# Between two mixture layers: evacuations and transposes moved up, three weight splits moved down, filler matmuls of another kind

## The chip, the core and the metric

The kernel runs on one core of a Trainium2 chip. The metric is the device time of one execution in microseconds (us), taken as the median of repeated runs. The core has five engines that run their own instruction streams and wait for each other through semaphores: TensorE (PE, with its weight loads shown as PEld), VectorE (DVE), ScalarE (ACT), GpSimd (POOL) and SyncE (SP), which here only issues DMAs. [...]

## What is computed

Three layers follow each other. An attention with a window of 32 and 32 global tokens gives 4 * (512 + 32) = 2176 tokens of 512 numbers, which the kernel handles as 17 tiles of 128. A mixture layer with a rational activation follows, then a layer with eight experts of which each token takes the one with the highest logit:

```
h = x @ w_in;  g = P(h) / (Q(h) + 1e-06);  x2 = g @ w_out           # first mixture layer
logits = normed(x2) @ normed(expert_emb).T / tau
expert_idx = argmax(logits);  gate_w = softmax(logits)[expert_idx]
for e in range(8):                                                   # second mixture layer
    mask = expert_idx == e
    out[mask] = gate_w[mask] * (relu(x2[mask] @ w1[e]) @ w2[e])
```

## The kernel before

The matrix products run in a three-term form: each float32 operand is split into a high part (rounded to fp32r) and a low part (the rest), and hi*hi, hi*lo and lo*hi are added. So every weight has to be split before it is used: ACT copies out the high part, DVE or POOL subtracts it to get the low part.

**The first mixture layer** (`moe1`) runs over blocks of tokens (`BLOCKS`, two of 512 tokens and three of 384) and slices of the hidden width. `gemm1` makes h, `poly`, `inv` and their kin make g on ACT, DVE and POOL, and `gemm2` adds to four accumulators in PSUM. When a token tile's sum is complete, `evac` (L1029) adds it on DVE to x2, and `final` writes x2 to DRAM (L1040, on SP's queue), transposes it on PE (L1043, four 128x128 transposes into tile tp) and copies the transpose out on ACT (L1050).

**Logits and ranks.** When a block has all its transposes, `logits` multiplies by the expert embeddings on PE (L1073) and ACT copies the result to `part` (L1078); `logits2` folds it into tile lp (L1084). A generator `pick` then does the block's ranks on DVE: maximum (L280, tile zm), one-hot (L281 to L289), running counts by matmuls of constants on PE (L294 to L298), then ranks (L309 to L321). `next(g)` runs it one step on; `for _ in g` runs it to its end. `norm` (L1058) sums squares on ACT; `norms` turns them into lengths (L331 to L342).

**After the last slice** (n = NK, L1165 on) this is written out by hand. Three token tiles (14, 15, 16) still have to be evacuated and transposed, and the ranks of blocks 2, 3 and 4 have to be done in their order, since each block's counts (`cum`) go on from the one before.

**The weights of expert 0 and 1.** In the same stretch the second layer's first weights are split. They come in eight chunks of 512 KB in the staging buffers `stg`: 0 to 3 are w1, 4 to 7 are w2. `first_hi` (L1226, ACT) makes the high part of a chunk, `first_lo` (L1231, DVE) the low part. For the chunks in `EARLY` = (0, 2) `first_lo` also starts the load of expert 1's chunk into the buffer just freed (L1233, on SP's queue). The others' low parts of w2 are made by DVE after the second layer has begun (L1624).

**Routing** (`route`) finishes the last `pick`, places each expert's tokens in slots (`place`, L489 to L508), and looks up by 17 small matmuls (`table`, L480) which token sits in which slot. From that come idx (L459) for the first gather of 128 rows of x2 by POOL's indirect DMA (L514), and scat (L463) for the scatters. `warm` (L468) puts transposes of the identity on PE ahead of and behind the table, whose results nobody reads.

**The second mixture layer** (`moe2`) is one critical block in which each engine has its own program with hand-placed semaphores. Every engine enters it through one branch (L1736, SP through a NO_OP at L1266) that waits for everything that came before: each DMA queue's semaphore at its last value, and each engine's. Then PE transposes the first gathered rows (L1373, d_x), runs 6 more transposes of `warm` (called at L1453), and multiplies (L1418 for a half-filled unit, L1404 for a full one, tile d_h; L1444 the second product, tile d_o). DVE turns the table's second use into gates (L1609 to L1613) and makes low parts (L1571); POOL makes others (L1676).

Nothing but the order in the source decides the order on each engine here; waits between engines are derived from what is read and written.

Of the kernel before, what the change touches and what calls it, by code (L numbers as in the profile page):

```python
# [19 lines left out]
P = 128  # L20
# [64 lines left out]
class Kernel:  # L85
# [331 lines left out]
    def route(self):  # L417
        tc, nc = self.tc, self.nc
        V, T = nc.vector, nc.tensor
        NS = NSLOT  # L420
        self.idx = self.wpool.tile([P, NS], I32, name="idx")
        self.scat = self.wpool.tile([P, NS], I32, name="scat")
        self.gate = self.big.tile([P, NS], F32, name="gate")
        self.tab = self.wpool.tile([1, NROW * NU], I32, name="tab")
        sel = self.wpool.tile([P, NTILE * NS // 2], F32, name="sel")
        self.sel = sel.bitcast(F16).rearrange("p (a b) -> p a b", b=NS)
        self.gs = sel[:, 0:3 * NS].rearrange("p (a b) -> p a b", b=NS)

        def run(gens, steps=10 ** 9):
            while gens and steps:  # L430
                g = gens.pop(0)
                if next(g, run) is not run:
                    gens.append(g)
                steps -= 1

        with ExitStack() as ctx:
            rp = ctx.enter_context(tc.tile_pool(name="r_sb", bufs=1))
            last = self.psteps.pop()
            while self.total is None:
                next(last)  # L440
            nu = rp.tile([P, E], I32, name="nu")
            ub = rp.tile([P, E], F32, name="ub")
            od = rp.tile([1, E], I32, name="od")
            tail = chain(self.nsteps, self.gates())
            wb = self.bank("s", "wb")
            self.warm(wb, 20)
            run([self.place(rp, nu, ub, od), last, islice(tail, 7)])
            rhs = self.table_rhs(self.xgt, 1)
            self.table_mul(V, rhs, 0, self.tok)
            t = self.lp[:, TB:TB + NS]  # L450
            self.table(T, t, rhs)
            self.warm(wb, 36)
            back = [self.slots(rp, ub, nu, od), tail]
            run(back, 3)

            up = rp.tile([P, NS], F32, name="up")
            none = rp.tile([P, NS], F32, name="none")
            V.tensor_scalar(up, t, 0.0, -1.0, ALU.is_gt, ALU.mult)
            V.scalar_tensor_tensor(self.idx, t, float(MID), up, ALU.add, ALU.add)  # L459
            self.gather(nc.gpsimd, 0, 0)  # L460
            run(back)
            V.tensor_scalar(none, t, 0.0, float(OOB), ALU.is_equal, ALU.mult)
            V.tensor_tensor(self.scat, self.idx, none, ALU.add)  # L463

    def warm(self, out, n):

        for _ in range(n):
            self.nc.tensor.transpose(out[:, 0:P], self.ident, self.ident)  # L468

    def table_rhs(self, t, n):  # L470
        return t[:, 0:NTILE * n * NSLOT // 2].bitcast(F16).rearrange("p (a j b) -> p a j b", j=n, b=NSLOT)
# [47 lines left out]
    def attention(self, ctx):  # L519
# [315 lines left out]
        }  # L835
        warm = one.tile([P, 512], F32R, name="warm")
        nc.scalar.copy(warm, vgs[0].rearrange("p a b c -> p (a b c)"))

        def heat(d, n):
            for _ in range(n):  # L840
                nc.tensor.matmul(d, warm[:, 0:P], warm, start=True, stop=True)
# [151 lines left out]
    def moe1(self, ctx, kctx, xctx):  # L993
# [8 lines left out]
        def gemm2(k):  # L1002
            g, (t0, n), f = k
            gh, gl = G.pop(k)
            wh, wl = self.w[f, 1]
            grp = GROUPS[g]
            first, last = f == grp[0], f == grp[-1]
            for i in range(n // P):
                tt = t0 // P + i
                if first:  # L1010
                    acc[tt] = self.bank("o", "o")
                o = acc[tt]
                gs = slice(i * P, (i + 1) * P)
                nc.tensor.matmul(o, gh[:, gs], wh[:, DM:], start=first, stop=False)  # L1014
                nc.tensor.matmul(o, gh[:, gs], wl[:, DM:], start=False, stop=False)  # L1015
                nc.tensor.matmul(o, gl[:, gs], wh[:, DM:], start=False, stop=last)  # L1016
                if last:
                    done.append((g, tt, o))

        def evac(g, tt, o):  # L1020
            if g == 0:
                (nc.scalar.copy if tt % 2 else nc.vector.tensor_copy)(self.x2[tt], o)
            elif tt % 2 and g < len(GROUPS) - 1:
                nm = ("junk", "part")[tt // 2 % 2]
                x = wk.tile([P, DM], F32, tag=nm, name=nm, bufs=1)
                nc.scalar.copy(x, o)
                nc.gpsimd.tensor_tensor(self.x2[tt], x, self.x2[tt], ALU.add)
            else:
                nc.vector.tensor_tensor(self.x2[tt], o, self.x2[tt], ALU.add)  # L1029
            if g == len(GROUPS) - 1:  # L1030
                fin.append(tt)

        def bank(nm):
            if n == NK:
                turn.append(turn.pop(0))
            return self.bank("s" if turn[0] else "t", nm)

        def final(tt):
            x2 = self.x2[tt]
            nc.sync.dma_start(self.x2_dram[tt * P:(tt + 1) * P, :], x2)  # L1040
            tp = bank("tp")
            for c in range(NDC):
                nc.tensor.transpose(tp[:, c * P:(c + 1) * P], x2[:, c * P:(c + 1) * P], self.ident)  # L1043
            bi, (a, b) = block_of(tt)
            if tt == a:

                old = BLOCKS[(bi - 1) % 3][0] // (2 * P)
                XT[bi] = self.st_raw if bi == 0 else [t.rearrange("p a b -> p (a b)") for t in pair[old:old + 2]]
            j = tt - a
            nc.scalar.copy(XT[bi][j // 2][:, j % 2 * DM:(j % 2 + 1) * DM], tp)  # L1050
            late.append(tt)
            if tt == b - 1:
                full.append(bi)

        def norm():
            for tt in late:
                junk = wk.tile([P, 512], F32, tag="junk", name="junk", bufs=1)
                nc.scalar.activation(junk, self.x2[tt], AF.Square, accum_out=self.ss[:, tt:tt + 1])  # L1058
            late.clear()

        def block_of(tt):
            bi = next(i for i, x in enumerate(BLOCKS) if tt * P < sum(x))
            return bi, (BLOCKS[bi][0] // P, sum(BLOCKS[bi]) // P)

        def logits(bi):

            w = BLOCKS[bi][1]
            xt = XT.pop(bi)
            tp = bank("lt")[:, :w]
            for i in range(0, w, 2 * P):  # L1070
                x = xt[i // (2 * P)].rearrange("p (a b) -> p a b", b=DM)[:, 0:min(2, (w - i) // P)]
                for c in range(NDC):
                    nc.tensor.matmul(  # L1073
                        tp[c * WIN:(c + 1) * WIN, i:min(i + 2 * P, w)], self.ent[:, c], x[:, :, c * P:(c + 1) * P],
                        start=True, stop=True, tile_position=(0, c * WIN),
                    )
            part = wk.tile([P, 512], F32, tag="part", name="part", bufs=1)[:, :w]
            nc.scalar.copy(part, tp)  # L1078
            return part
# [19 lines left out]
        done, fin, full, late, parts, XT, turn = [], [], [], [], [], {}, [0, 1, 1]  # L1099
# [7 lines left out]
        for n in range(PRE, NK):  # L1107
# [52 lines left out]
            g, blk, f = ks[n - LAG + 1]  # L1160
# [18 lines left out]
        g = self.psteps[-1]  # L1179
        while next(g) is None:  # L1180
            pass
        self.first_lo((0, 2))
        part = logits(full.pop())
        norm()
        gemm2(ks[-1])
        next(g)
        for _ in g:
            pass
        for d in done:
            evac(*d)  # L1190
        self.first_hi((1, 3))
        self.psteps.clear()
        logits2(bl - 1, part)
        g = self.psteps.pop()
        while next(g) is None:
            pass
        while fin:
            final(fin.pop(0))
        for _ in g:
            pass  # L1200
        self.first_lo((1, 3))
        part = logits(full.pop())
        norm()
        self.nsteps = self.norms()
        next(self.nsteps)
# [46 lines left out]
    def moe2(self, ctx):  # L1252
# [5 lines left out]
        po = [pp.tile([P, 512], F32, name=f"d_o{i}") for i in range(2)]  # L1258
# [7 lines left out]
        with tc.tile_critical():  # L1266
# [20 lines left out]
            def base(nm, j, half):  # L1287
                return sum(incs[nm][h] for _, h in order[:order.index((j, half))])
# [45 lines left out]
            with nc.Block() as block:  # L1334
# [27 lines left out]
                def _(E):  # L1362
# [13 lines left out]
                    def second(j):  # L1376
                        either(E, two[j], lambda: tx_(j, 1), lambda: E.sem_inc(tx[1], 1))
# [72 lines left out]
                    n = val(ET.PE, 6, 0, NU_MIN, NU)  # L1450
                    ahead(0)
                    second(0)
                    self.warm(po[0], 6)  # L1453
                    for j in range(NU):
                        if 0 < j < NU - 1:
                            ahead(j + 1)
# [283 lines left out]
```

## Time and profile before

| | us |
|---|---|
| median of 3 runs (901.66 to 907.16) | 904.59 |
| the profiled execution | 896.24 |
| its span, first to last instruction | 894.3 |
| in it, from the last product of the first layer to the first expert product | 578.9 to 603.7 |

The page's first section gives each engine's busy time as a share of the span. The chain of waits is followed back from the last instruction, at each step to what released it. A timeline row gives start, duration, engine, line, operation, output and inputs, count, and in brackets the idle time before it and what ended that. In the table by windows the column PEclk is the granted clock. "Issue" is a wait for nothing that the profile shows.

### The profile page before, as it was taken

The numbers are of one execution on the slowest core, as the hardware profiler recorded it, in microseconds if no ns is written. First come the engines' busy times: TensorE is split into PE (matmuls) and PEld (weight loads), VectorE is DVE, ScalarE is ACT, GpSimd is POOL, SyncE is SP. The second block draws the span as 40 slices with busy tenths as digits, with TensorE's granted clock in tenths as the row PEclk, the third lists the DMA queues.
The fourth block names the chain that finished last, engine by engine and source line by source line (L and its number), as shares of the span: only waits on it lengthen the run. The fifth ranks groups of instructions, "written<-read, shape, count | busy, mean of one in ns | idle before, by whom it ended". The sixth has DMA issues, their size and how long they took to land.

```text
span 894.3 us, 17479 instructions
## 1 busy us (share of the span) xinstructions
PE 835.5 (93%) x6015; PEld 711.2 (80%) x6015; DVE 621.3 (69%) x1288; ACT 542.1 (61%) x1180; POOL 412.4 (46%) x381
## 2 busy tenths in 40 slices
PE   6888989889999999999999999969899999999994
PEld 5666777668988888888888888758778889898983
DVE  2767777787898888889887868889645982213620
ACT  5566766667888888887888778746234731113211
POOL 4333333454555676776667533325545861013400
PEclk9999999999999999999999999979899999999998
DMA  6655655301111111111100140428825982011100
GB/s 164 140 125 136 139 134 128 84 25 49 48 48 47 31 41 48 48 47 48 48 25 1 48 141 36 157 83 292 282 76 190 316 294 86 25 49 50 39 18 14
DMA packets 106502, 84.97 MB, mean 95 GB/s; under 512 B 79175, under 2 KB 87367, under 8 KB 106384
## 3 DMA queue, kind: packets, MB, share of 16 engines
q1 hardware_dynamic: 102864, 73.18, 28.0%
q0 software_dynamic: 3520, 10.23, 3.3%
q8 instruction: 72, 1.18, 0.6%
q14 instruction: 46, 0.38, 0.1%
HBM read 74.47 MB, written 10.22 MB: 95 GB/s over the span
## 4 chain that ended last, share of the span: by engine, by line
PE 81%; DVE 5%; issue 4%; SPq 3%; DMA 3%; POOL 1%; ACT 1%; DVEq 0%; POOLq 0%; ACTq 0%
PE h L942 21%; PE d_o L1444 14%; PE d_h L1404 10%; PE o L1014 7%; PE o L1016 7%; PE o L1015 7%; PE d_h L1418 4%; PE sb L649 3%; DMA q<-q_l 2%; PE gob L820 1%; SPq L552 1%; PE d_x L1373 1%; PE tb L708 1%; PE lb L761 1%; PE xb L729 1%
## 5 line engine op out<-in xcount | busy, mean ns | idle before, releaser
L942 PE MATMUL h<-xhi,wr 128*128 128x384 f32 (+1 forms) x480 | 145.0, 363 | 3.2 <-DVE t L971 3.2
L951 POOL TENSOR_TENSOR u<-u,v 128x384 f32<-128x384 f32 (+1 forms) x80 | 90.4, 1130 | 123.9 <-ACT v L949 97.5
L1444 PE MATMUL d_o<-wr,xlo 128*128 (+1 forms) x528 | 127.2, 399 | 4.4 <-issue 3.9
L1444 PEld LDWEIGHTS d_o<-wr,xlo 128*128 128x128 f32 x528 | 100.0, 192 | 27.3 <-issue 5.2
L942 PEld LDWEIGHTS h<-xhi,wr 128*128 128x128 f32 x480 | 89.5, 189 | 12.7 <-DVE t L971 3.6
L980 POOL TENSOR_TENSOR gl<-t,gh 128x384 fp32r<-128x384 f32 (+1 forms) x80 | 90.8, 1135 | 19.1 <-ACT gh L979 7.5
L1404 PEld LDWEIGHTS d_h<-xlo,wr 128*128 128x128 f32 x768 | 93.1, 192 | 2.7 <-issue 2.1
L1404 PE MATMUL d_h<-xlo,wr 128*128 128x256 f32 x768 | 93.5, 283 | 1.7 <-issue 1.7
L942 PE MATMUL h<-xlo,wr 128*128 128x384 f32 (+1 forms) x240 | 86.5, 360 | 0.0
L1512 ACT ACTIVATE xlo<-d_h 128x512 fp32r<-128x512 f32 x32 | 19.1, 596 | 105.3 <-PE d_h L1404 94.7
L1014 PE MATMUL o<-wr,gh 128*128 128x512 f32 x204 | 81.2, 398 | 0.0
L1016 PE MATMUL o<-wr,gl 128*128 128x512 f32 x204 | 80.0, 392 | 0.0
L1015 PE MATMUL o<-wr,gh 128*128 128x512 f32 x204 | 79.8, 391 | 0.0
L1676 POOL TENSOR_TENSOR wr<-xhi,wr 128x1024 f32 x21 | 62.5, 2988 | 28.4 <-ACT wr L1501 18.8
L1571 DVE TENSOR_TENSOR wr<-xhi,wr 128x1024 f32 x35 | 72.8, 2126 | 3.8 <-issue 3.6
L948 ACT ACTIVATE u<-h,ab 128x384 f32<-128x384 f32 (+1 forms) x80 | 49.7, 621 | 32.7 <-PE h L942 18.4
L956 DVE TENSOR_TENSOR t<-t,h 128x384 f32<-128x384 f32 (+1 forms) x80 | 48.5, 606 | 29.3 <-ACT t L950 28.3
L1662 POOL DMA_INDIRECT out<-xlo,scat x22 | 26.0, 1180 | 90.1 <-DVE xlo L1604 88.8
L676 ACT ACTIVATE pr<-pr,nm 128x160 f32<-128x160 f32 x128 | 53.0, 425 | 15.7 <-DVE rs L686 10.4
L963 ACT ACTIVATE v<-u,one 128x384 f32<-128x384 f32 (+1 forms) x80 | 53.4, 668 | 12.4 <-POOL u L951 12.0
L1604 DVE TENSOR_SCALAR xlo<-d_o,gate 128x512 f32<-128x512 f32 x22 | 16.4, 748 | 63.1 <-PE d_o L1444 63.1
L690 POOL TENSOR_TENSOR pr<-pr,rs 128x512 f32<-128x512 f32 x32 | 38.8, 1231 | 44.7 <-DVE rs L687 44.7
(290 smaller groups left out, 2000.3 us busy)
## 6 DMA issues: line engine op xcount, KB each, us to landing
xhi<-w SPq DMA_DIRECT2D x64, 512.0 KB, 4.8
st_raw<-w_in SPq DMA_DIRECT2D x16, 512.0 KB, 3.8
st_raw<-w_out SPq DMA_DIRECT2D x16, 512.0 KB, 3.5
x_dram<-x SPq DMA_DIRECT2D x17, 256.0 KB, 2.1
k<-k_l SPq DMA_DIRECT2D x32, 128.0 KB, 3.4
q<-q_l SPq DMA_DIRECT2D x32, 128.0 KB, 3.9
va<-v_l SPq DMA_DIRECT2D x32, 96.0 KB, 2.6
vb<-v_l SPq DMA_DIRECT2D x32, 96.0 KB, 2.6
```

Of the source, the lines that this page charges most:

```text
L676: nc.scalar.activation(pr[:, i], pr[:, i], AF.Exp, bias=nm[:, i:i + 1], scale=SCALE, accum_out=sums[:, i:i + 1],)
L942: nc.tensor.matmul(h, w[:, cs], x, start=(i == 0), stop=(i == 3 * NDC - 1))
L951: nc.gpsimd.tensor_tensor(u, u, v, ALU.add)
L963: nc.scalar.activation(v, u, AF.Ln, bias=self.one)
L980: nc.gpsimd.tensor_tensor(gl, t, f32(gh), ALU.subtract)
L1014: nc.tensor.matmul(o, gh[:, gs], wh[:, DM:], start=first, stop=False)
L1015: nc.tensor.matmul(o, gh[:, gs], wl[:, DM:], start=False, stop=False)
L1016: nc.tensor.matmul(o, gl[:, gs], wh[:, DM:], start=False, stop=last)
L1404: r = nc.tensor.matmul(o, w(0, par, b, sl), xs[a][:, c], start=(i == 0), stop=(i == len(steps) - 1))
L1444: r = nc.tensor.matmul(po[t], ht[a][h][:, c, t * P:(t + 1) * P], w(1, par, b, sl), start=(h == c == a == b == 0), stop=(h == a == 1 and c ...
L1571: E.tensor_tensor(l_, stg[i], f32(h_), ALU.subtract).then_inc(ld, 1)
L1676: E.tensor_tensor(l_, stg[i], f32(h_), ALU.subtract).then_inc(lp, 1)
```

## The change

Four pieces, all between the layers:

1. At the end of `moe1` the three evacuations and the three `final` come ahead of the ranks of block 2, where the evacuations stood behind these and the transposes behind the counts of block 3. On ACT the copies of the transposes (L1050) now stand ahead of the high parts of chunks 1 and 3. The second `logits` is called ahead of the ranks of block 3.
2. The low parts of chunks 2, 1 and 3 move from the ranks to the end of `route`, behind scat. With chunk 2 goes its load of expert 1's weights.
3. `warm` issues matmuls of the bfloat16 constant `ones`, 512 columns each, in place of 128-column transposes of the float32 identity: 9 ahead of the table in place of 20, 13 behind it in place of 36.
4. The 6 at the start of the block are dropped.

```diff
-            self.warm(wb, 20)
+            self.warm(wb, 9)
             run([self.place(rp, nu, ub, od), last, islice(tail, 7)])
...
             self.table(T, t, rhs)
-            self.warm(wb, 36)
+            self.warm(wb, 13)
...
             V.tensor_tensor(self.scat, self.idx, none, ALU.add)
+            self.first_lo((2, 1, 3))
 
     def warm(self, out, n):
 
         for _ in range(n):
-            self.nc.tensor.transpose(out[:, 0:P], self.ident, self.ident)
+            self.nc.tensor.matmul(
+                out, self.ones, self.ones[:, None, :].to_broadcast([P, 4, P]), start=True, stop=True)
...
-        self.first_lo((0, 2))
+        self.first_lo((0,))
         part = logits(full.pop())
         norm()
         gemm2(ks[-1])
-        next(g)
+        for d in done:
+            evac(*d)
+        while fin:
+            final(fin.pop(0))
+        self.first_hi((1, 3))
         for _ in g:
             pass
-        for d in done:
-            evac(*d)
-        self.first_hi((1, 3))
         self.psteps.clear()
         logits2(bl - 1, part)
         g = self.psteps.pop()
         while next(g) is None:
             pass
-        while fin:
-            final(fin.pop(0))
+        part = logits(full.pop())
         for _ in g:
             pass
-        self.first_lo((1, 3))
-        part = logits(full.pop())
         norm()
...
                     second(0)
-                    self.warm(po[0], 6)
                     for j in range(NU):
```

What this does to the engines' order is shown at three places. In the names, xhi_6376, xhi_6378, xhi_6872 and xhi_6874 are the staging buffers of chunks 0, 2, 1 and 3. Lines of the changed kernel are one or two off.

DVE, from the low part of chunk 0 to the maximum of block 3, before:

```order
L1231 TENSOR_TENSOR wr_6892<-xhi_6376,wr_88 128x1024
L1231 TENSOR_TENSOR wr_6892<-xhi_6378,wr_88 128x1024
L309 TENSOR_TENSOR eq<-lp,oh 128x24
L311 TENSOR_REDUCE pf<-eq 128x3
L313 CAST rank<-pf 128x3
L315 TENSOR_SCALAR rq<-rank 128x3
L316 TENSOR_SCALAR rank<-rank 128x3
L318 CAST pf<-rank 128x3
L321 TENSOR_SCALAR xlo_6558<-ip,pf 128x128 x3
L1029 TENSOR_TENSOR x_14_3177<-o,x_14_3177 128x512 x2
L1029 TENSOR_TENSOR x_16_3178<-o,x_16_3178 128x512
L280 TENSOR_REDUCE zm<-lp 128x3
```

and in the changed kernel:

```order
L1231 TENSOR_TENSOR wr_6892<-xhi_6376,wr_88 128x1024
L1031 TENSOR_TENSOR x_14_3177<-o,x_14_3177 128x512 x2
L1031 TENSOR_TENSOR x_16_3178<-o,x_16_3178 128x512
L309 TENSOR_TENSOR eq<-lp,oh 128x24
L311 TENSOR_REDUCE pf<-eq 128x3
L313 CAST rank<-pf 128x3
L315 TENSOR_SCALAR rq<-rank 128x3
L316 TENSOR_SCALAR rank<-rank 128x3
L318 CAST pf<-rank 128x3
L321 TENSOR_SCALAR xlo_6558<-ip,pf 128x128 x3
L280 TENSOR_REDUCE zm<-lp 128x3
```

The three evacuations moved up over the ranks of block 2, and the low part of chunk 2 is gone from here.

DVE, the end of the routing and the branch into the block of the second layer, before:

```order
L364 CAST gp_322<-gr 128x17
L366 TENSOR_TENSOR gp_323<-gr,gp_322 128x17
L462 TENSOR_SCALAR none<-lp 128x32
L463 TENSOR_TENSOR scat<-idx,none 128x32
L1736 UNCONDITIONAL_BRANCH
```

and in the changed kernel:

```order
L366 TENSOR_TENSOR gp_323<-gr,gp_322 128x17
L462 TENSOR_SCALAR none<-lp 128x32
L463 TENSOR_TENSOR scat<-idx,none 128x32
L1231 TENSOR_TENSOR wr_6892<-xhi_6378,wr_88 128x1024
L1231 TENSOR_TENSOR wr_6892<-xhi_6872,wr_88 128x1024
L1231 TENSOR_TENSOR wr_6892<-xhi_6874,wr_88 128x1024
L1735 UNCONDITIONAL_BRANCH
```

Three low parts stand between scat and the branch.

SP, the last DMAs ahead of the block with the semaphores that each waits for (DMAHW0 to 7 belong to SP's queue, DMASW0 to the gather), before:

```order
L1040 DMA x_dram<-x_12_3176 128x512 [waits DMAHW1_49,DVE_49]
L1233 DMA xhi_6376<-w 128x1024 [waits DMAHW2_49,DVE_49]
L1233 DMA xhi_6378<-w 128x1024 [waits DMAHW3_49,DVE_49]
L1040 DMA x_dram<-x_14_3177 128x512 [waits DMAHW4_49,DVE_49]
L1040 DMA x_dram<-x_14_3177 128x512 [waits DMAHW5_49,DVE_49]
L1040 DMA x_dram<-x_16_3178 128x512 [waits DMAHW6_49,DVE_49]
L1266 NO_OP [waits DMAHW2_49,DMAHW1_49,DMAHW3_49,DMAHW0_49,DMAHW4_49,DMASW0_49,DMAHW5_49,DVE_49,DMAHW6_49,PE_49,DMAHW7_49,Activation_49,Pool_49]
```

and in the changed kernel:

```order
L1233 DMA xhi_6376<-w 128x1024 [waits DMAHW2_49,DVE_49]
L1042 DMA x_dram<-x_14_3177 128x512 [waits DMAHW3_49,DVE_49]
L1042 DMA x_dram<-x_14_3177 128x512 [waits DMAHW4_49,DVE_49]
L1042 DMA x_dram<-x_16_3178 128x512 [waits DMAHW5_49,DVE_49]
L1233 DMA xhi_6378<-w 128x1024 [waits DMAHW6_49,DVE_49,Activation_49]
L1266 NO_OP [waits DMAHW2_49,DMAHW1_49,DMAHW3_49,DMAHW0_49,DMAHW4_49,DMASW0_49,DMAHW5_49,DVE_49,DMAHW6_49,PE_49,DMAHW7_49,Activation_49,Pool_49]
```

The load of expert 1's chunk 2 moved behind the last writes of x2 and is now the last DMA ahead of the NO_OP; it counts up DMAHW6, for which the NO_OP and every engine's branch wait.

## Rows read from the trace of the kernel before

**Rows 1.** The page's first section: busy us (share of the span) xinstructions.

```profile
PE 835.5 (93%) x6015; PEld 711.2 (80%) x6015; DVE 621.3 (69%) x1288; ACT 542.1 (61%) x1180; POOL 412.4 (46%) x381
```

**Rows 2.** The chain of waits in order of time: start us, us, what.

```profile
581.00 1.79 DVE x L1029 x3
...
586.01 2.27 DVE wr L1231 x2
...
595.92 3.89 DMA xlo<-x_dram,idx
...
600.74 1.03 PE d_x L1373 x4
...
602.53 1.51 PE d_o L468 x6
...
611.00 2.32 DVE gate L1613
```

**Rows 3.** Timeline of DVE between the layers.

```profile
579.09 0.17 DVE L309 TENSOR_TENSOR eq<-lp,oh 128x24 f32<-128x24 f32 x1
...
580.92 1.88 DVE L1029 TENSOR_TENSOR x<-o,x 128x512 f32<-128x512 f32 x3
582.72 0.17 DVE L280 TENSOR_REDUCE zm<-lp 128x3 f32<-128x24 f32 x1
...
588.20 0.18 DVE L280 TENSOR_REDUCE zm<-lp 128x3 f32<-128x24 f32 x1
...
589.77 0.25 DVE L334 RECIPROCAL q<-nr 128x17 f32<-128x17 f32 x1
...
597.47 0.19 DVE L463 TENSOR_TENSOR scat<-idx,none 128x32 int32<-128x32 int32 x1
```

**Rows 4.** Timeline of ACT in the same stretch.

```profile
578.61 1.98 ACT L1226 CAST wr<-xhi 128x1024 fp32r<-128x1024 f32 x2
582.35 1.78 ACT L1050 COPY x<-tp 128x512 f32<-128x512 f32 x3 [1.77 <-PE tp L1043]
584.97 0.48 ACT L1078 COPY part<-lt 128x384 f32<-128x384 f32 x1 [0.83 <-PE lt L1073]
...
587.95 0.22 ACT L332 ACTIVATE nr<-nr 128x17 f32<-128x17 f32 x1
```

**Rows 5.** Timeline of PE from the last logits into the second layer.

```profile
585.50 0.83 PE L1084 MATMUL lp<-fold,part 128*128 128x8 f32 x6 [0.65 <-ACT part L1078]
...
589.40 4.51 PE L468 MATMUL wb<-ident 128*128 128x128 f32 x20
...
594.42 4.13 PE L468 MATMUL wb<-ident 128*128 128x128 f32 x36
...
603.70 4.86 PE L1418 MATMUL d_h<-wr,xlo 128*128 128x512 f32 x12
...
609.12 3.01 PE L1418 MATMUL d_h<-wr,xlo 128*128 128x512 f32 x12
...
616.58 3.93 PE L1444 MATMUL d_o<-wr,xlo 128*128 128x512 f32 x16 [0.39 <-DVE xlo L1595]
```

**Rows 6.** Table by windows: window, length, busy us of PE, PEld, DVE, ACT, POOL, then PEclk, DMA share, GB/s.

```profile
594.00:594.50 0.50, 0.50 (x18) 0.50 (x18) 0.50 (x6) 0.00 (x0) 0.00 (x0) 0.96 0.00 0
...
600.50:601.00 0.50, 0.26 (x2) 0.27 (x3) 0.34 (x1) 0.00 (x0) 0.00 (x0) 0.87 0.00 0
...
607.50:608.00 0.50, 0.50 (x3) 0.36 (x3) 0.50 (x2) 0.50 (x1) 0.50 (x1) 0.80 0.91 270
```

**Rows 7.** Line L1233, loads of expert 1's chunks 0 and 2: issue to landing.

```profile
DMA to landing us min/median/max: 3.4/4.0/4.5
```

**Rows 8.** Line L878, loads of the same 512 KB in the first layer.

```profile
DMA to landing us min/median/max: 3.4/3.5/6.3
```

**Rows 9.** Timeline of POOL, the low parts of chunks 2 and 3 of expert 1.

```profile
607.46 5.80 POOL L1676 TENSOR_TENSOR wr<-xhi,wr 128x1024 f32 x2 [2.59 <-ACT wr L1501]
```

## The prediction

> **What bounds the kernel now.** I read the page's first section, then the chain of waits between the layers, then the timelines of DVE, ACT and PE for that stretch, then the granted clock by windows. TensorE is busy for 93% of the span [rows 1], so the kernel as a whole is bound by it; the change touches none of that work, only the stretch between the layers and the 6 transposes after it, where PE waits for others. There the chain runs on DVE: evacuations (1.79), low parts of chunks 1 and 3 (2.27), ranks and placing, then the first gather, 3.89 from its issue to its landing, and then PE's first transposes at 600.74 [rows 2]. The gather lands at 595.92 + 3.89 = 599.81, and PE starts 0.93 later: that is the cost of entering the block. Scat is done at 597.66 [rows 3], 2.15 ahead of the landing, so the gather alone holds the entry.
>
> **The change part by part, first the order of the ranks.** I walk down DVE's timeline in the new order. The rank tail of block 2 starts at 579.09, behind two low parts; one of these takes about 1.2 (half of 2.27, and the start of its successor), so with only chunk 0's there DVE is free at 577.9. The evacuations take 1.88 and end at 579.8; the rank tail takes 580.92 - 579.09 = 1.83 and ends at 581.6. Block 3's maximum then stands at 581.6 in place of 582.72 [rows 3]: 1.1 gained, the low part that left. Block 3's ranks run from 582.72 to the low parts at 586.01 [rows 2, 3], 3.3, so DVE comes to block 4's maximum at 584.9. Before, the two low parts stood there and it began at 588.20 [rows 3]: **3.3 gained**, if its inputs are there.
>
> They come over ACT and PE, which is what could take their place. The first copy of a transpose starts 582.35 - 580.92 = 1.43 after the first evacuation [rows 3, 4], so at 579.3, and the third ends 582.35 + 1.78 - 580.92 = 3.21 after it, at 581.1. Now ACT's two high parts stand behind them and ahead of the copy of the logits: 1.98 [rows 4], to 583.1. The logits' product on PE runs beside that. The copy takes 0.48 [rows 4] and the fold 0.83 [rows 5]: ready at about 584.5, 0.4 ahead of DVE. The lengths end 587.95 + 0.22 - 584.97 = 3.2 after the copy's start [rows 4], at 586.3; DVE asks for them at 589.77 - 3.3 = 586.5 [rows 3]. Both fit, by 0.2 to 0.4; I take 3.3 and keep 2.7 as the low end, and 1.1, what the departed low part alone brings, as the floor should ACT not deliver. Everything behind, with the gather and scat, moves by the same amount: gather landed at 596.5, scat at 594.4.
>
> **The low parts behind the routing.** DVE does chunk 2's first, 594.4 to 595.6, then those of 1 and 3 to 598.0. What ends last is neither: with chunk 2 goes a load of 512 KB, which SP can issue only once the low part has been read, and every engine's branch waits for its semaphore. Nothing else is queued on SP ahead of it. Lines that move the same 512 KB land in 3.4 to 4.5 [rows 7] and, with little else under way, 3.5 at the median [rows 8]. The longest of them is 6.3 [rows 8]; I keep 4.5 as the high end, since the stretch has only the gather beside it, and take 3.5. With 0.1 for SP that is 595.6 + 0.1 + 3.5 = 599.2, against 599.81 before: **the entry moves by 0.6, not by 3.3**. The gather's landing is replaced by that of the load. POOL's five small table instructions run while DVE makes the low part and may delay it by one of theirs; I allow 0.1, and am left with 0.5.
>
> **The filler.** Nobody reads its result; it must only be out of PE's way and serve the clock. Ahead of the table: 9 matmuls of 512 columns. The expert's 12 of the same width took 4.86 at mostly the low clock and 3.01 at the high one with other work in between [rows 5], so one costs 0.41 at the low clock and not over 0.25 at the high one. 9 cost 3.7 or 2.3 in place of 4.51; they begin when the counts end and are over before the table's operand is ready, as the 20 transposes were. The 13 behind the table take 3.3 to 5.3 in place of 4.13, and end by 597 where the entry is at 599.2. Both cost nothing.
>
> The clock is where they could bring something. In the trace it rose to full at the start of the window at 594.0, after PE had done nothing but transposes of the identity since 589.40; it fell at 600.9, with PE idle from 598.55 to 600.74, and rose again at 607.6 [rows 5, 6]. So the transposes of before do raise the clock. What they did not do is carry it over the entry, where PE stands still. With the change PE stops at 597 at the latest, likely near 594.4, and stands still until 600.1, longer than before. So I expect the low clock at the entry again, and no gain.
>
> [...]
>
> **The six transposes in the block.** They took 1.51, from 602.53 [rows 2], and the first expert product began at 603.70 [rows 5]. Taken away, PE waits for ACT's and DVE's copies of the transposed rows instead, so at most 0.7 could be gained. Behind it stands another wait: PE's second product pauses at 616.58 for DVE [rows 5], DVE comes there from its gates (2.32 for a tiny operation [rows 2]), and these last as long as POOL's low parts, to 607.46 + 5.80 = 613.26 [rows 9]. That chain starts from the entry on ACT and POOL, not from PE. So an earlier PE waits longer there. I take 0, with 0.4 to either side: the clock may also rise later since PE starts to work later.
>
> **The sum.** 0.5 on the entry and 0 elsewhere: 896.24 - 0.5 = 895.7 on the profiled execution's basis. That execution lies 0.9% under the median of the timed runs; I carry the difference over: 904.59 - 0.5 = **904.1**.
>
> **Rivals.** *The entry is paid, not gained.* The new route loses where the old one had slack: the entry is later than before as soon as the ranks' gain is below 1.2 + 0.1 + 3.5 - 2.15 = 2.65. With a gain of 2.7 and a landing of 4.5 the entry is 1.0 later, 905.6; with the floor of 1.1 and 4.5 it is 2.6 later, 907.2. For it speak the thin slack of 0.2 to 0.4 behind ACT's high parts, and that landings are up to 4.5; against it that each step of the walk has its row.
>
> *The clock survives the entry.* Then the first transposes take 0.6 in place of 1.03 and the first 12 products about 3.0 in place of 4.86 [rows 2, 5], 2.3 together: 901.8 with the forecast's entry. [...]
>
> *The load doesn't hold the entry*, since it lands sooner than any of its size did or the branches don't wait for it: the whole 3.3 is gained, 901.3, with the clock 899.0. Against it stands the branch's list of semaphores, where that load's is named.
>
> *Nothing moves at all*, because the ranks were not bound by DVE: then the late load alone makes the entry 2.65 later, which is the first rival's high end.
>
> **How the numbers follow.** Forecast, entry earlier by 0 to 1: 0.60. Entry paid: 0.22. Clock survives: 0.08. Load doesn't hold: 0.07, with the clock too 0.03. A measurement of this kernel can tell about 0.5%, 4.5 us, from no change; only the last case gets there by itself. The runs of before lie 5.5 apart, so a median of three can be off by some 2 on either side; that gives most of what I put outside. Faster by over 0.5%: 0.10, within: 0.81, slower: 0.09. The range goes from the clock's case less 2 to the entry paid in full: 899.5 to 907.5.
>
> **What would show it.** In the changed trace, zm of block 4 about 3.3 earlier against the last first-layer product, and part's copy on ACT right behind the high parts; the load of chunk 2 issued just behind its low part and landing last, 2 to 3 after the gather; the first transposes on PE about 0.9 behind that landing; PE's clock at the low level there. I am wrong if the chain still names the gather ahead of the entry, if the clock is full at the first expert products, or if ranks of block 4 wait for ACT.

## The result and the profile after

The changed kernel takes **891.38 us** in the median (885.16 to 893.89, 4 runs), the kernel before 904.85 in the runs beside it (901.66 to 907.16): a ratio of 0.985, interval 0.981 to 0.989. The prediction of 904.1, range 899.5 to 907.5, was wrong: 13 us came off where half a microsecond was forecast.

The two profiled executions, cut into stretches by the ends of PE's products:

| stretch, us | before | after | difference |
|---|---|---|---|
| start to the last product of the first layer | 578.94 | 586.08 | +7.14 |
| from there to the second layer's first transposes (entry) | 21.80 | 20.94 | -0.86 |
| to the end of unit 0's second product | 19.77 | 19.53 | -0.24 |
| **to the end of the last second product** | **262.57** | **254.24** | **-8.33** |
| to the end of the span | 11.20 | 11.21 | 0 |

A unit is up to 256 tokens of one expert; there are 14. In the first stretch PE has the same program in both, and in the eleven other traces of this study, which share it, it ends between 578.99 and 583.36; it differs from one execution to the next. In this pair it hides most of the gain: the spans are 894.3 and 892.0. The forecast was about the second and third rows, and these came out near what it said (0.5 and 0). The gain is in the fourth, where the change touches no line.

The page's first section of after: 40 matmuls and 40 weight loads less than in [rows 1], as the diff has it.

```profile
PE 833.0 (93%) x5975; PEld 705.3 (79%) x5975; DVE 621.6 (70%) x1288; ACT 541.9 (61%) x1180; POOL 415.6 (47%) x381
```

The chain of waits of after, where [rows 2] had the gather: start, us, what.

```profile
601.34 1.20 DVE wr L1231
...
602.59 3.62 DMA xhi<-w
...
607.02 1.13 PE d_x L1373 x4
```

The late load now holds the entry. Its issue follows its low part at once, it takes 3.62 (forecast: 3.5), and PE starts 0.81 behind its landing. The timelines of DVE and ACT, as [rows 3, 4]:

```profile
591.95 0.17 DVE L280 TENSOR_REDUCE zm<-lp 128x3 f32<-128x24 f32 x1
...
601.20 0.19 DVE L463 TENSOR_TENSOR scat<-idx,none 128x32 int32<-128x32 int32 x1
601.31 3.49 DVE L1231 TENSOR_TENSOR wr<-xhi,wr 128x1024 fp32r<-128x1024 f32 x3
```

```profile
588.28 1.99 ACT L1226 CAST wr<-xhi 128x1024 fp32r<-128x1024 f32 x2
590.18 0.48 ACT L1080 COPY part<-lt 128x384 f32<-128x384 f32 x1
```

Block 4's maximum stands 591.95 - 586.08 = 5.87 behind the first layer's end, where it was 588.20 - 578.94 = 9.26 [rows 3]: 3.4 gained, forecast 3.3. The logits' copy follows the high parts without a gap. PE, as [rows 5]:

```profile
593.15 3.79 PE L469 MATMUL wb<-ones 128*128 128x512 bf16 x9
...
598.17 2.97 PE L469 MATMUL wb<-ones 128*128 128x512 bf16 x13
607.02 1.11 PE L1373 MATMUL d_x<-ident,xlo 128*128 128x128 f32 x4 [5.89 <-SPq L1266]
609.72 4.86 PE L1418 MATMUL d_h<-wr,xlo 128*128 128x512 f32 x12 [1.59 <-ACTq L1491]
...
615.21 3.01 PE L1418 MATMUL d_h<-wr,xlo 128*128 128x512 f32 x12
```

The first 12 products take 4.86 as before. The granted clock says why; the records of both traces have it at 1.0 (full) or at 0.5 and nowhere else. The table by windows, as [rows 6]:

```profile
597.50:598.00 0.50, 0.26 (x11) 0.26 (x11) 0.50 (x5) 0.00 (x0) 0.00 (x0) 1.00 0.00 0
606.50:607.00 0.50, 0.00 (x0) 0.00 (x0) 0.04 (x1) 0.00 (x0) 0.00 (x0) 0.50 0.00 0
...
614.00:614.50 0.50, 0.50 (x5) 0.23 (x3) 0.50 (x1) 0.50 (x1) 0.50 (x1) 1.00 1.02 393
```

The clock is full at the 13 matmuls behind the table (1.00 from 596.64 to 603.47) and low at the entry (0.50 to 613.71), as forecast, and full again by 614 (1.00).

**The fourth stretch.** In the waits of PE with the releaser "issue" (nothing that the profile shows) the two traces differ. The longest of them, before:

```profile
635.79 13.97 PE L1444 MATMUL d_o<-wr,xlo 128*128 x48 [3.33 <-issue]
664.46 11.77 PE L1404 MATMUL d_h<-xlo,wr 128*128 128x256 f32 x96 [1.71 <-issue]
...
775.07 0.65 PE L1373 MATMUL d_x<-ident,xlo 128*128 128x128 f32 x4 [1.84 <-issue]
870.27 5.72 PE L1418 MATMUL d_h<-wr,xlo 128*128 x24 [1.57 <-issue]
```

and after:

```profile
726.34 10.63 PE L1444 MATMUL d_o<-wr,xlo 128*128 x46 [1.01 <-issue]
...
808.13 5.71 PE L1418 MATMUL d_h<-wr,xlo 128*128 x24 [1.67 <-issue]
```

(The 1.01 stands two products into its group.) All of PE's pauses over 0.1 in this stretch come to 9.58 before and 4.71 after. The first one before also cost clock: the windows of before show it low from the end of the pause and full again 7 us later, and its 48 products took 13.97 where the same 48 take 11.15 in after.

```profile
635.00:635.50 0.50, 0.00 (x0) 0.00 (x0) 0.50 (x2) 0.50 (x2) 0.00 (x0) 0.50 1.03 353
...
642.00:642.50 0.50, 0.50 (x4) 0.42 (x3) 0.00 (x0) 0.00 (x0) 0.00 (x0) 1.00 1.05 406
```

4.87 of pauses and 2.82 of clock make 7.7 of the 8.33. What PE pauses for stands in the view of the DMA queues. In the window 632 to 634, at the start of the 3.33, before fetches one packet of a queue named instruction (packets, MB, share):

```profile
q8 instruction: 1, 0.02, 2.9%
```

Its packets are all 16,384 bytes, and between two of them in the straight code of the first layer PE issues 127 matmuls and 127 weight loads on average: the window between two neighbours in before (PE and PEld are the first two counts; one or two lie on the edges).

```profile
349.90:375.00 25.10, 25.10 (x125) 22.32 (x124) 22.47 (x40) 21.68 (x43) 17.72 (x17) 1.00 0.13 43
```

So this queue brings PE's own program, some 256 instructions a packet. The packets and the pauses belong together in all thirteen traces of this study: each of the 41 pauses of 0.65 us and more in the fourth stretch ends 1.2 to 1.8 us after a packet has come in whole (2.3 in the three ahead of unit 1's second product). A moment taken at random in this stretch lies 1.2 to 1.8 us behind a packet in only 7 to 8% of cases. And the stretch has 33 packets in every one of these traces, so that the kernels differ not in how many come but in whether they come in time.

The second layer is full of branches: a unit is whole or half, an expert's weights lie in one of two halves, and the code of each case stands in a row. That gave the theory: **the change takes 80 instructions out ahead of the second layer, and so all of its code stands elsewhere with regard to the packets; more of its branches now hit packets that are there already.**

### The profile page after: what moved, and what is told of

Same layout as the page of the kernel before. It is cut to its first block, busy times and chain, and to the rows that moved or that the text cites. A ratio compares the mean times of both kernels' runs of the same rounds, so it can differ in the third digit from the quotient of the medians.

```text
span 892.0 us, 17395 instructions
## 1 busy us (share of the span) xinstructions
PE 833.0 (93%) x5975; PEld 705.3 (79%) x5975; DVE 621.6 (70%) x1288; ACT 541.9 (61%) x1180; POOL 415.6 (47%) x381
## 4 chain that ended last, share of the span: by engine, by line
PE 82%; DVE 5%; SPq 4%; DMA 3%; issue 3%; ACT 2%; POOL 1%; DVEq 0%; POOLq 0%; ACTq 0%
PE h L944 21%; PE d_o L1444 13%; PE d_h L1404 10%; PE o L1016 7%; PE o L1018 7%; PE o L1017 7%; PE d_h L1418 4%; PE sb L651 3%; DMA q<-q_l 2%; PE gob L822 1%; SPq L554 1%; PE d_x L1373 1%; ACT pr L678 1%; PE lb L763 1%; PE tb L710 1%
## 5 line engine op out<-in xcount | busy, mean ns | idle before, releaser
L1444 PE MATMUL d_o<-wr,xlo 128*128 (+1 forms) x528 | 124.2, 393 | 1.9 <-issue 1.5
L1444 PEld LDWEIGHTS d_o<-wr,xlo 128*128 128x128 f32 x528 | 98.0, 188 | 23.3 <-issue 2.6
L952 ACT ACTIVATE t<-h,ab 128x384 f32<-128x384 f32 (+1 forms) x80 | 57.2, 715 | 0.0
```

The costliest lines, as they stand in the source:

```text
L952: nc.scalar.activation(t, h, AF.Identity, bias=self.ab[:, 2:3], scale=self.ab[:, 3:4])
L1444: r = nc.tensor.matmul(po[t], ht[a][h][:, c, t * P:(t + 1) * P], w(1, par, b, sl), start=(h == c == a == b == 0), stop=(h == a == 1 and c ...
```

## Experiments: order or place

The rival is that the order of the ranks and the late load bring the gain, through other work beside the second layer. Four kernels on one chip: each of the two again, the change with the old place, the old order with the new place. The edit of after_at_before cuts the filler, of nearly as many columns in all (11,236 in place of 11,264), into 62 pieces, so that PE's program behind it has as many instructions ahead of it as in before:

```diff
-            self.warm(wb, 9)
+            self.warm(wb, 20, 115, 2)
...
-            self.warm(wb, 13)
+            self.warm(wb, 42, 79, 2)
...
-                out, self.ones, self.ones[:, None, :].to_broadcast([P, 4, P]), start=True, stop=True)
+                out[:, 0:reps * cols], self.ones, self.ones[:, None, 0:cols].to_broadcast([P, reps, cols]), start=True, stop=True)
```

before_at_after is the kernel before, its 56 transposes replaced by 16 of the 512-column matmuls (the 6 in the block stay), which is 80 instructions less; order, low parts and loads are those of before:

```diff
-            self.warm(wb, 20)
+            self.fill(wb, 6)
...
-            self.warm(wb, 36)
+            self.fill(wb, 10)
```

> The kernel before, unchanged, to see how far two sets of runs of one program lie apart, and whether the stalls of its second layer return. Theory (place of PE's code): the waits of PE without a releaser stand at the same places as in the first trace (3.3 us ahead of the second unit's d_o at L1444, and 1.6 to 1.8 ahead of three later groups), and the time from the first d_o that waits for DVE to the last d_o is 266 us within 1.5. Rival (chance): they stand elsewhere and that time differs by several us. Ratio 1.00 either way.

> The changed kernel, unchanged, a second time. Theory (place of code): the second layer from the first waiting d_o to the last d_o takes 258 us within 1.5, as in its first trace; the whole is 1% to 1.5% faster than before. Rival (chance): that time is anywhere between 258 and 266, and the ratio comes back towards 1.00.

> The changed kernel with its filler cut into more and narrower pieces (20 of 230 columns and 42 of 158 in place of 9 and 13 of 512), the same columns in all, so that PE's code of the second layer stands exactly where it stands in the kernel before. Theory (place of code): the stalls of before come back at their places, the second layer takes about 266 us again, and the whole is 7 to 9 us slower than the changed kernel, about 0.99 to 1.00 of before. Rival (the change's own order and its clock bring the gain): no difference from the changed kernel, 0.985.

> The kernel before with its 56 filler transposes replaced by 6 and 10 matmuls of 512 columns of ones, so that PE's code of the second layer stands where it stands in the changed kernel; order of ranks, low parts and the 6 transposes in the block are those of before. Theory (place of code): the second layer takes about 258 us, and the whole is 0.985 to 0.992 of before, though nothing of the new order is in it. Rival (the order brings the gain): 1.00.

| kernel | place | median us | ratio to before | entry | fourth stretch, profiled | pauses in it |
|---|---|---|---|---|---|---|
| before_again | before's | 898.27 | 0.9977 (0.9948 to 1.0006) | 22.12 | 263.66 | 11.39 |
| after_at_before | before's | 900.44 | 0.9972 (0.9944 to 1.0001) | 20.71 | 269.74 | 13.41 |
| after_again | after's | 889.35 | 0.986 (0.982 to 0.990) | 21.10 | 257.08 | 6.37 |
| before_at_after | after's | 891.28 | 0.9875 (0.9839 to 0.991) | 21.85 | 256.94 | 6.05 |

The place decides, in both directions. The whole change without its change of place is not to be told from before: at 0.9972 it lies where before_again does, the same program as before, at 0.9977. The old order with the new place has the gain.

The expectations in microseconds were met less well. They counted from the product of unit 0 that waits for DVE and put 266 for before's place and 258 for after's; by the same count it took 267.6 in before_again, 273.7 in after_at_before, 261.0 in after_again and 260.9 in before_at_after. The places part as expected, but after_again missed its band by 1.5, and after_at_before is 11.1 slower than after_again where 7 to 9 were expected. The traces show part of it: after_at_before has the clock low for 13.65 us of the fourth stretch, and the pause in unit 6 of after's place isn't always 1.01. In after_again it was:

```profile
723.07 11.95 PE L1444 MATMUL d_o<-wr,xlo 128*128 x46 [3.27 <-issue]
```

The pauses go with the place, too. after_at_before has those of before, at the same instructions:

```profile
637.59 13.54 PE L1444 MATMUL d_o<-wr,xlo 128*128 x48 [4.12 <-DVE wr L1570]
665.97 13.26 PE L1404 MATMUL d_h<-xlo,wr 128*128 128x256 f32 x96 [1.84 <-issue]
...
781.58 0.65 PE L1373 MATMUL d_x<-ident,xlo 128*128 128x128 f32 x4 [1.86 <-issue]
878.45 5.72 PE L1418 MATMUL d_h<-wr,xlo 128*128 x24 [1.55 <-issue]
```

and before_at_after has those of after:

```profile
725.98 12.24 PE L1450 MATMUL d_o<-wr,xlo 128*128 x46 [2.94 <-issue]
809.35 5.73 PE L1424 MATMUL d_h<-wr,xlo 128*128 x24 [1.66 <-issue]
```

(The first row of after_at_before names DVE. It is the same pause: in before, before_again and after_at_before PE goes on 2.34, 2.35 and 2.34 us after a packet has come, and the first two rows name no engine. The length differs, 3.33, 3.50 and 4.12, as the packet starts 0.06, 0.20 and 0.83 behind the start of the pause.)

## Experiments: can the place be reckoned

If the theory holds, the pauses follow from the program alone. I listed PE's blocks with their number of instructions from the program as built, walked them for the 14 units of this input (whole or half, first or second half of the weights), and let a packet of 256 be fetched when PE enters the one before it, or when a branch lands outside; so a pause can also stand a few instructions behind a branch that lands near a packet's end. This way of fetching is an assumption of the walk. The packets of before and after fit it: behind each of their six pauses over 1 us one starts 0.60 to 2.33 us after PE goes on, and the next 10.5 to 14.7 us after that one. What sets a fetch off isn't shown. A fetch was put at 3.3 us while weights still load and at 1.7 after, as in the rows above. One number was fitted, where a packet begins, to the pauses of before and of after and to their sums within 2. The walk isn't printed here; its figures stand in the expectations, written before the three kernels ran. It then gives 4.3 us for after's place and 10 for before's, and a period of 256 instructions, 128 pairs. Three kernels test it: the changed kernel, its filler of nearly as many columns (11,200 to 11,308) cut into 150, 106 and 140 pieces in place of 22. The edit is as above with other numbers, after_plus128, after_plus84 and after_plus118 in turn:

```diff
+            self.warm(wb, 40, 115, 1)
+            self.warm(wb, 110, 60, 1)
...
+            self.warm(wb, 30, 77, 2)
+            self.warm(wb, 76, 88, 1)
...
+            self.warm(wb, 40, 115, 1)
+            self.warm(wb, 100, 66, 1)
```

> The changed kernel with its 22 filler matmuls cut into 150 narrower ones of together as many columns: PE's program behind them stands 256 instructions later, which in the traces is just what one 16 KB packet of PE's instruction queue holds (127 matmuls with their 127 weight loads between two packets). Place of the code, with a period of one packet: the stalls fall where they fall in the changed kernel, behind the second product of unit 6 and ahead of unit 10, some 4 to 6 us in all; ratio to before 0.984 to 0.989, about 890 us. Rival, a lower number of PE instructions is what helps: 216 more than in the kernel before must then be slower than before, 905 or more. Rival, order and late load: as the changed kernel, 890.

> The changed kernel with its filler cut into 106 pieces of together as many columns: PE's program stands 168 instructions later than in the changed kernel. Place of the code: walking the branches of the second layer with packets of 256 instructions, of which only the next one is fetched ahead, I count stalls at eight places, worst of all places, 14 us together at 3.3 us a fetch while weights load and 1.7 after, against 4.3 in the changed kernel and 10 in before. So about 10 slower than the changed kernel, 900, with lost clock up to 905; ratio to before 0.997 to 1.005. The stalls stand ahead of d_o of unit 1, of d_h of units 3, 5, 10 and 13 and at the transposes behind d_h of units 7 and 9. Rival, order and late load: as the changed kernel, 890.

> The changed kernel with its filler cut into 140 pieces of together as many columns: 236 instructions later, that is 20 short of a whole packet. Place of the code: the best place of the walk, 2.8 us of stalls against 4.3 in the changed kernel; the one behind the second product of unit 6 shrinks from about 2.5 to 0.5 to 1, that ahead of unit 10 stays 1.7. About 1.5 to 3 faster than the changed kernel, 887 to 889; ratio to before 0.981 to 0.987. Rival, order and late load: as the changed kernel, 890.

| kernel | walk's pauses | measured, profiled | fourth stretch | median us | ratio to before |
|---|---|---|---|---|---|
| after_plus128 | 4.3 | 4.94 | 255.68 | 891.63 | 0.9909 (0.9871 to 0.9947) |
| after_plus84 | 14 | 11.85 | 262.22 | 898.94 | 0.9994 (0.9967 to 1.0022) |
| after_plus118 | 2.8 | 4.48 | 255.83 | 889.71 | 0.9881 (0.9847 to 0.9915) |

256 instructions more change nothing that these runs can tell, which was the sharpest test: 88 matmuls and 88 weight loads more than before, 176 instructions (the expectation miscounts them as 216), and still faster than before. The page counts a packet more than before's and after's 72:

```profile
q8 instruction: 73, 1.20, 0.6%
```

After_plus84 loses the whole gain, within the band of its expectation. Its longer pauses, each at a place that the expectation had named (ahead of d_h of units 3, 5, 10 and 13, and at or just behind the transposes of units 7 and 9):

```profile
659.29 11.77 PE L1404 MATMUL d_h<-xlo,wr 128*128 128x256 f32 x96 [0.88 <-issue]
...
698.92 5.72 PE L1418 MATMUL d_h<-wr,xlo 128*128 x24 [3.53 <-issue]
...
749.28 0.65 PE L1373 MATMUL d_x<-ident,xlo 128*128 128x128 f32 x4 [1.77 <-issue]
797.27 11.19 PE L1444 MATMUL d_o<-wr,xlo 128*128 x48 [0.96 <-issue]
810.17 5.74 PE L1418 MATMUL d_h<-wr,xlo 128*128 x24 [1.71 <-issue]
871.31 5.73 PE L1418 MATMUL d_h<-wr,xlo 128*128 x24 [1.90 <-issue]
```

The one that I had named in the first units isn't there; PE had waits for other engines of 0.60 and 0.40 there. In after_plus118 the pause in unit 6 is down from 2.13 in after_plus128 to 0.31, as the walk said, but it has small ones that the walk doesn't know, and the whole is 4.48, not 2.8. Two of them, 0.54 ahead of unit 5 and 0.37 ahead of unit 11, end 1.6 and 1.5 us behind a packet and so are fetches, too; the 0.61 ahead of unit 4's second product, which all thirteen traces have with 0.45 to 0.61, ends over 4 us behind the last packet and is something else. The walk tells which place is bad, and not the last microsecond. Its time is 1.9 under that of after_plus128, which these runs can't tell from nothing. The ratios of after_plus128 and after_plus118, and of early_load below, lie 0.1 to 0.2% above their expected bands; against the 902.02 that before took beside the first set, on another chip, in place of 899.94, all three would lie within.

## Experiments: the steps of the forecast

**Does the load hold the entry?** early_load moves the low part of chunk 2 back:

```diff
-            self.first_lo((2, 1, 3))
+            self.first_lo((1, 3))
...
-        self.first_lo((0,))
+        self.first_lo((0, 2))
```

> The changed kernel with the low part of chunk 2, and with it the load of the next expert's chunk 2, back ahead of the ranks; only the low parts of chunks 1 and 3 stay behind the routing. PE's program is the same instruction for instruction. Theory, the load's landing holds the entry: without it the gather's landing holds it. The ranks come 1.2 later than in the changed kernel, all behind them too; from the end of the first layer's last product to the first transposes of the second layer it takes 19.6 us in place of 20.9, and the low parts of 1 and 3 end just before the gather lands. 1.3 faster in that stretch, ratio to before 0.982 to 0.988. Rival, the load's landing isn't what the branch waits for: the ranks' 1.2 is lost, 22.1 us.

```profile
600.17 1.12 PE L1373 MATMUL d_x<-ident,xlo 128*128 128x128 f32 x4 [3.57 <-SPq L1266]
```

The first layer's last product ends at 580.44, so the entry takes 19.73: 19.6 was expected, 22.1 by the rival, and the changed order otherwise has 20.7 to 21.1. So the load did hold it. Without it the gather lands at 599.09 and DVE's last low part ends at 599.15, about a microsecond ahead of PE's first transposes. The median is 890.14 (ratio 0.989, 0.9851 to 0.9929), not to be told from after_plus128's 891.63 beside it.

**Is the filler worth its clock?** no_filler cuts its 22 matmuls to 8 columns; combined has early_load's order and after_plus118's place; combined_clock is combined with the last 100 pieces twice as wide, up to the entry. The calls of no_filler, then the last call of combined and of combined_clock:

```diff
+            self.warm(wb, 9, 8, 1)
+            self.warm(wb, 13, 8, 1)
...
-            self.warm(wb, 100, 66, 1)
+            self.warm(wb, 100, 66, 2)
```

> The changed kernel with its 22 filler matmuls cut to 8 columns each, next to no work, PE's program in the same place. The prediction's step said that the filler costs nothing and brings nothing for the clock at the entry: the clock is low at the first transposes and products with it and without it, and the time is that of the changed kernel within 1 us, ratio to before 0.984 to 0.992. Rival, the filler holds part of the clock up: the routing's matmuls and the entry are slower, by 1 to 3 us, 891 to 894.

> The early load of early_load together with the filler in 140 pieces of after_plus118, PE's best place. Theory (place of the code, and the load's landing at the entry): both gains add, 19.7 us from the first layer's last product to the second layer's first transposes in place of 20.9, and 2.8 us of stalls in place of 4.3; 2.5 faster than the changed kernel, 887 to 888; ratio to before 0.981 to 0.988. Rival, the earlier entry is given back behind it by a wait of the second product for DVE: as after_plus118, 889 to 890.

> As combined, but the 100 pieces behind the table are of 132 columns in place of 66, so that PE works until about 0.5 us ahead of the entry. The clock should then still be full there: the first transposes 0.65 in place of 1.12, the first 12 products of expert 0 some 3.0 in place of 5. The prediction's step said that an earlier PE waits longer at the second product of the first unit, for DVE: then that wait grows from under 0.5 to 2 to 3, and the time is that of combined within 0.5. Rival, the clock is worth its time: 2.3 faster than combined, 885.

no_filler takes 890.97 (0.9899, 0.9856 to 0.9942), its entry 20.81. Its clock is low where after's was full, and nothing follows from it:

```profile
597.50:598.00 0.50, 0.00 (x0) 0.00 (x0) 0.50 (x1) 0.00 (x0) 0.50 (x1) 0.50 0.72 238
```

combined takes 887.79 (0.9871, 0.9833 to 0.991) and combined_clock 887.22 (0.9863, 0.9822 to 0.9903). First combined, then combined_clock:

```profile
601.06 1.12 PE L1373 MATMUL d_x<-ident,xlo 128*128 128x128 f32 x4 [3.22 <-SPq L1266]
603.76 4.34 PE L1418 MATMUL d_h<-wr,xlo 128*128 128x512 f32 x12 [1.58 <-ACTq L1491]
...
617.00 3.92 PE L1444 MATMUL d_o<-wr,xlo 128*128 128x512 f32 x16 [1.28 <-DVE xlo L1594]
```

```profile
594.58 5.91 PE L469 MATMUL wb<-ones 128*128 128x132 bf16 x100
601.33 0.66 PE L1373 MATMUL d_x<-ident,xlo 128*128 128x128 f32 x4 [0.84 <-PE wb L469]
603.57 4.32 PE L1418 MATMUL d_h<-wr,xlo 128*128 128x512 f32 x12 [1.59 <-ACTq L1491]
```

The transposes took 0.66 in place of 1.12, as at the full clock (0.65 in before), and PE began its products 2.24 after their start in place of 2.70. But the 12 products behind the 1.59 in which PE waited for ACT took 4.32 again, where 12 took 3.01 in before with the clock full, so that the case in which they run at full clock was not reached. The wait for DVE at the second product, which the expectation put at under 0.5 in combined and at 2 to 3 in combined_clock, was 1.28 and 0.78. The median moved by 0.6, which is nothing here.

The stretch from the first transposes to the end of unit 0's second product measures it best. In all thirteen profiles, with 6 transposes or none, with a full or a low clock at their start, it lies between 19.41 and 19.95. What PE saves there it mostly waits again for DVE.

combined and combined_clock have the two lowest medians of the study and are clearly ahead of before. Against the changed kernel (891.38 and 889.35) they are some 2 to 4 us lower, but they were not timed beside it: by the ratio to before, each beside its own runs, they are no better (0.9871 and 0.9863 against 0.985 and 0.986), and no_filler's 890.97 in the same set has runs that overlap with theirs. That they beat it isn't shown.

## Why the prediction was wrong

- **The order of the ranks**: right. 3.4 gained, 3.3 forecast, and ACT kept up.
- **The load holds the entry**: right, and shown by early_load. The entry came 0.86 earlier in place of 0.5: the landing, though it took 3.62 in place of 3.5, came 0.74 earlier against the first layer's end, as the ranks brought 3.4, and PE started 0.81 behind it in place of 0.93. No run shows the 0.1 that was allowed for POOL: in after, with POOL's table instructions beside the last three, one low part took 1.21 to 1.25, as in before.
- **The filler and the clock at the entry**: right in this: the clock is low at the first products with transposes (before: 0.50 from 600.87 to 607.70, products from 603.70), with real matmuls (after: 0.50 from 603.47 to 613.71, products from 609.72), and with next to none (no_filler: 0.50 at 606, products from 605.18). It did rise after the transposes of before, at 594.04, and after the matmuls of after, at 596.64, alike; in before_at_after, with 16 such matmuls, it stayed low from 587.18 to 611.07.
- **The six transposes at 0**: right, by the stretch that stays at 19.4 to 19.95.
- **The entry is paid**, the rival with 0.22: it didn't happen.
- **The sum, "0.5 on the entry and 0 elsewhere"**: the 0 elsewhere is the step that failed. Each removed matmul was priced by its own time. That 80 instructions stand no longer ahead of the second layer's code had no price at all, and it was nearly the whole result: 8.33 of the first pair's fourth stretch and 6.58 of the second's (before_again to after_again), and about 1.1% of the time between after_again and after_at_before, which do the same work. What is left up to the 1.5%, some 0.4%, is little more than the 0.2% by which two sets of runs of one program differ (before_again). "The change touches none of that work" was true of the work and not of the program that PE has to fetch, and a PE that is busy for 93% of the span isn't thereby bound by its work alone.

The rows to see it were in the trace of before: pauses of 3.33, 1.71, 1.84 and 1.57 with no releaser behind branches, in a stretch that the argument called bound by TensorE, and 72 packets of an instruction queue. They make some 8 us, and if these hang on the place of the code, a change in the number of PE's instructions can move the time by as much, to either side. With the walk, the forecast would have been 10 - 4.3 = 5.7 less of pauses and some clock with it; but the walk was fitted to the trace of after as well, so how much of this could have been had beforehand is open. Without it, the honest range was wider on both sides by some 8 us.

Left open: the small pause ahead of unit 4's second product, which no packet explains; and how much of the medians' 11 to 13 us beyond the pauses is clock lost behind them. In the profiles of before's place the clock was low for 3.41 to 13.65 us of the fourth stretch, in those of after's place for 0 to 3.41; the timed runs have no such rows.

## What to carry to other kernels

Before pricing an edit that adds or removes instructions ahead of branching code, list the engine's pauses with no releaser in that code and compare their times with the packets of its instruction queue; if they meet, the number of instructions is itself a term of the sum, of unknown sign until the branches are walked. When a timed change has moved a stage that it doesn't touch, undo its change of place alone (filler cut into more or fewer pieces of the same total) before believing in its order. And a tuned time may rest on such a place: the worst place tried here gave back all of the 1.5%. All of this was measured on one input, whose units decide which branches are taken.

## What the runs showed of the hardware

- PE's program comes in packets of 16,384 bytes, one to some 256 instructions, and a program longer by just that many behaves the same (891.63 us against 891.38 and 889.35; 88 instructions less than that cost 7.3 us).
- Where no DMA moved data (share 0.00), PE went on 1.4 to 1.8 us after a packet had come, and most of its pauses for one took 1.5 to 1.9 us. While weights loaded (share 0.67 and more) they took up to 3.5, and 4.1 with the one whose row names DVE.
- A pause can take the clock with it: in the 3.33 of before it fell and was low for 6.83 us, and 48 products took 13.97 in place of 11.15. It fell in or just behind nine others as well, of 1.80 (after_plus118) to 4.12 (after_at_before). It doesn't always: behind the 3.53 of after_plus84 it stayed full.
